# Output rows of the cosine layer in three runs a step instead of seven, and the softmax guard as a sum over column pairs

## Chip, cores and metric

One core of a Trainium2 chip. The metric is the device time of one execution in microseconds (us), the median of three runs. Engines: TensorE (PE, its weight loads are listed as PEld), VectorE (DVE), ScalarE (ACT), GpSimd (POOL), and SyncE (SP), which issues nearly all DMAs.

## The reference, cut to what matters

Windowed attention with 4 batches, 8 heads, 576 tokens and head size 64, then two feed-forward layers over the 2304 tokens of width 512:

```
scores = scale * q @ k.T + slope_h * -|i - j|   (only 0 <= i - j < 128, else -1e9)
e      = exp(scores - max(scores))
x      = (e / (sum(e) + 1e-9)) @ v
g      = x @ w_gate;  x = (g * sigmoid(g) * (x @ w_val)) @ w_out      (d_ff 1536)
h      = x @ w_in;    x = (h * cos(h)) @ w_out2                       (d_ff 2048)
```

All inputs are float32.

## The kernel before

Every float32 operand of the two layers is split in a high and a low part, and each product is three matmuls (high by high, high by low, low by high) that accumulate in PSUM (`mm3`, lines 83 to 86, and `prod`, lines 1009 to 1017). The order in which instructions are issued is written out by hand; each engine then works off its own list in that order and waits for the others by semaphores.

There are three stages.

**Attention** (loop of line 680). Work goes by items (a head and a block of 128 queries), mostly two to a group. For a group the scores are made on PE (`do_s`), bias and row minimum on DVE (`do_bias`, line 514), the exponential with its row sum on ACT (`do_exp`, line 523), then on DVE the guard, which adds 1e-9 to the sum (`do_guard`, line 529), and the reciprocal (`do_recip`, line 534); POOL scales the rows (`do_norm`, lines 546 and 547), PE transposes them (lines 556 and 566) and multiplies by v (line 624). A small tile `st` of 12 columns, one of eight that take turns, holds a group's statistics: columns 0 and 1 the row minima of its one or two items, columns 2 and 4 the sums of exp, column 3 what the tile was filled with at the start (1.0). The guard writes columns 5 to 7 from 2 to 4, the reciprocal columns 8 to 10. Between these steps matmuls of the first layer are issued on PE as filler (lines 84 to 86), and DVE, ACT and POOL split weights for it (line 167 on POOL).

**The rest of the first layer** (loop of line 1062), matmuls of 384 columns without a pause. The last lines of it also set up the third stage.

**The cosine layer** (loop of line 1222), which the change is about. The tokens are in 3 strips of 768 (two halves of `BW` = 384), the 2048 hidden channels in 8 pairs of 128-channel blocks per strip; a step `k` is one pair of one strip, 24 steps (`K2`). h of a step is a 2 by 2 block product, made with seven products (Winograd's form of Strassen's scheme) instead of eight. A slot `m` of the step is one product: six matmuls of 384 columns into a PSUM bank (`prod`). The pool `pm` has two banks; a product takes the one that was let go first. Product 6 accumulates on the bank of product 4 (`p7`), after DVE has read that one once. `take` then reads the product's bank: for m = 0 ACT copies it (line 1166); for all others DVE adds it to an earlier partial sum (line 1156). Products 1, 4, 5 and 6 each give a finished quarter of h, tile `c`, in which a chain begins (`cosine`, lines 1127 to 1147):

- ACT rounds h / 2 pi (two instructions, lines 1130 and 1131)
- DVE subtracts the multiple of 2 pi (two, lines 1134 and 1135)
- ACT takes absolute value and sine (lines 1137 and 1138)
- POOL multiplies by h (line 1140)
- ACT makes the high part `hh` (line 1144), DVE the low part `hl` (line 1146)

Each slot moves every live chain on by one of these parts (`slot_chains`, line 1149; two chains at most while k < 2), then issues what was put off (`flush`), one operation of the next strip's preparation if there is one (`bg`, from `make_xt`, lines 969 to 991: 18 operations, twice in the run, seven of each 18 on DVE, four on POOL), then `take`.

Behind `take` come the output rows. An output row (`out_rows`, line 1191) is g @ w_out2 for 128 tokens and one channel block: three matmuls of 512 columns (lines 84 to 86 again) that accumulate in one of six PSUM banks over all 16 blocks of a strip. A step has 12 rows, 2 blocks by 6 token groups, and those issued in step k belong to step k - 2. `PER` says how many rows stand behind each product:

```
PER = [2, 2, 2, 2, 2, 1, 1]
```

So PE alternates between products and rows seven times a step. There are no rows in steps 0 and 1, and no products in the two steps behind the last (24 and 25), which run rows alone. Behind the last row of a bank's strip, ACT (in the last strip also DVE) copies the bank out, and SP stores it. SP loads a product's weights (`load_ws`) seven products ahead and w_out2's (`load_wo`, in slot 1) about two steps ahead.

Of the kernel before, what the change touches and what calls it, by code (L numbers as in the profile page):

```python
# [13 lines left out]
ALU = mybir.AluOpType  # L14
# [14 lines left out]
def kernel(  # L29
# [12 lines left out]
    nc = tc.nc  # L42
# [165 lines left out]
    def flush():  # L208
        for _ in range(len(post)):
            post.popleft()()  # L210
# [213 lines left out]
        nc.vector.memset(t, 0.0)  # L424
    stats = [const.tile([128, 12], F32, name=f"st{j}") for j in range(8)]
    for t in stats:
        nc.vector.memset(t, 1.0)
    stat_turn = [0]
    pth = {}
    slopes = [2.0 ** (-8.0 * (h + 1) / H) for h in range(H)]  # L430
# [37 lines left out]
    for u in range(U):  # L468
# [4 lines left out]
        for j in range(0, NI, 2):  # L473
            g = list(range(u * NI + j, u * NI + min(j + 2, NI)))
# [4 lines left out]
    def width(i):  # L479
        return 128 if i == 0 else 192 if i == NB else 256  # L480
# [44 lines left out]

    def do_guard(g):
        st = ST[g[0]][0]
        c = 2 * len(g) - 1
        nc.vector.tensor_scalar(st[:, 5:5 + c], st[:, 2:2 + c], 1e-9, None, ALU.add)

    def do_recip(g):
        st = ST[g[0]][0]
        c = 2 * len(g) - 1
        nc.vector.reciprocal(out=st[:, 8:8 + c], in_=st[:, 5:5 + c])  # L534

    def folded(n):

        u, _, i = items[n]
        return u >= NP and i < NB

    def do_norm(n):
        w = width(items[n][2])
        (st, m), e = ST.pop(n), E[n]
        if folded(n) and w == 256:
            w = 128
            nc.gpsimd.tensor_tensor(out=e[:, :w], in0=e[:, :w], in1=e[:, w:2 * w], op=ALU.add)
        nc.gpsimd.tensor_scalar(e[:, :w], e[:, :w], st[:, 8 + 2 * m:9 + 2 * m], 1.0, ALU.mult, ALU.mult)  # L547

    def do_t(g):
        u, h, i = items[g[0]]  # L550
# [129 lines left out]
    for n in range(N + PVS + 2):  # L680
# [19 lines left out]
        if ended(NORM):  # L700
            do_guard(ended(NORM))
        if turned:
            do_t(turned)
        if v1 is not None:
            if idx == TT0:
                g = turned
                prep_tail_t(v1, TT[g[0]] if g else ps_t.tile([128, 512], F32, tag="t", name="t"))
        if ended(NORM):
            do_recip(ended(NORM))
            for m in ended(NORM):  # L710
                do_norm(m)
# [283 lines left out]
    K2 = NS * NPAIR  # L995
# [5 lines left out]
    def load_ws(upto):  # L1001
        while wnext[0] < min(upto, 7 * K2):
            k, m = divmod(wnext[0], 7)
            t = wsp[0].tile([128, 2, 256], F32R, tag="ws", name="ws")
            nc.sync.dma_start(out=f32(t), in_=wid[k % NPAIR][:, m])
            WS[k, m] = t
            wnext[0] += 1

    def prod(k, m, ps, start=True):
        w = WS.pop((k, m))  # L1010
        hi, lo = (x[m] for x in XT[k // NPAIR])
        for kk in range(2):
            c = slice(kk * 128, (kk + 1) * 128)
            o, wh, wl, xh_, xl_ = ps[:, :BW], w[:, 0, c], w[:, 1, c], hi[:, kk], lo[:, kk]
            nc.tensor.matmul(out=o, lhsT=wh, rhs=xh_, start=start and kk == 0, stop=False, skip_group_check=True)  # L1015
            nc.tensor.matmul(out=o, lhsT=wh, rhs=xl_, start=False, stop=False, skip_group_check=True)  # L1016
            nc.tensor.matmul(out=o, lhsT=wl, rhs=xh_, start=False, stop=kk == 1, skip_group_check=True)  # L1017
# [81 lines left out]
    def new_bank(n):  # L1099

        if n < 12 and n % 3:
            return pl2.tile([128, 512], F32, tag="l2", name="l2")
        return pm.tile([128, 512], F32, tag="pm", name="pm")
# [23 lines left out]
    def cosine(k, fi, half, h):  # L1127

        a = ap_.tile([128, BW], F32, tag="a", name="a")
        nc.scalar.activation(out=a, in_=h, func=AF.Copy, scale=INV2PI, bias=MAGIC)  # L1130
        nc.scalar.activation(out=a, in_=a, func=AF.Copy, bias=-MAGIC)
        yield
        r = rp.tile([128, BW], F32, tag="r", name="r")
        nc.vector.scalar_tensor_tensor(out=r, in0=a, scalar=-C1, in1=h, op0=ALU.mult, op1=ALU.add)
        nc.vector.scalar_tensor_tensor(out=r, in0=a, scalar=-C2, in1=r, op0=ALU.mult, op1=ALU.add)  # L1135
        yield
        nc.scalar.activation(out=r, in_=r, func=AF.Abs)  # L1137
        nc.scalar.activation(out=r, in_=r, func=AF.Sin, bias=halfpi, scale=-1.0)  # L1138
        yield
        nc.gpsimd.tensor_tensor(out=r, in0=r, in1=h, op=ALU.mult)  # L1140
        yield
        hi = hp.tile([128, BW], F32R, tag="hh", name="hh")
        lo = hp.tile([128, BW], F32R, tag="hl", name="hl")
        nc.scalar.copy(out=hi, in_=r)
        yield
        nc.vector.tensor_tensor(out=lo, in0=r, in1=f32(hi), op=ALU.subtract)
        HS[k, fi, half] = hi, lo

    def slot_chains(most):

        for c in list(live)[:most]:
            if next(c, "end") == "end":
                live.remove(c)

    def add(out, a, ps):
        nc.vector.tensor_tensor(out=out, in0=ps[:, :BW], in1=a, op=ALU.add)  # L1156
# [3 lines left out]
    def take(k, m, ps):  # L1160

        def new(pool, tag):
            return pool.tile([128, BW], F32, tag=tag, name=tag)
        if m == 0:
            cur["q"] = new(tp, "q")
            nc.scalar.copy(out=cur["q"], in_=ps[:, :BW])  # L1166
        elif m == 1:
            c = new(cp, "c")
            add(c, cur["q"], ps)
            live.append(cosine(k, 0, 0, c))  # L1170
        elif m == 2:
            add(cur["q"], cur["q"], ps)
        elif m == 3:
            cur["r"] = new(tp, "r5")
            add(cur["r"], cur["q"], ps)
        else:
            c = new(cp, "c")
            fi, half, base = {4: (1, 1, "r"), 5: (0, 1, "r"), 6: (1, 0, "q")}[m]
            add(c, cur[base], ps)
            live.append(cosine(k, fi, half, c))  # L1180

    def load_wo(k):
        if k < K2:
            for fi in range(2):
                t = wop.tile([128, 2, 512], F32R, tag="wo", name="wo")
                nc.sync.dma_start(out=f32(t), in_=wod[2 * (k % NPAIR) + fi])
                WO[k, fi] = t
# [3 lines left out]
    def out_rows(k, fi, j):  # L1191

        s, p = divmod(k, NPAIR)
        first, final = p == 0 and fi == 0, p == NPAIR - 1 and fi == 1
        if first:
            sums[j] = (pl2.tile([128, 512], F32, tag="l2", name="l2") if j < 5 else
                       pl1a.tile([128, 512], F32, tag="l1", name="l1"))
        hi, lo = HS[k, fi, j // 3]
        w = WO[k, fi]
        c = slice(j % 3 * 128, (j % 3 + 1) * 128)  # L1200
        mm3(sums[j], hi[:, c], lo[:, c], w[:, 0], w[:, 1], first, final)
        if final:
            def ev(ps=sums[j], row=s * 6 + j):
                o = op_.tile([128, 512], F32, tag="o", name="o")
                if j % 2 and s == NS - 1:
                    nc.vector.tensor_copy(out=o, in_=ps)
                else:
                    nc.scalar.copy(out=o, in_=ps)
                nc.sync.dma_start(out=out[row * 128:(row + 1) * 128, :], in_=o)
            post.append(ev)  # L1210
# [3 lines left out]
    def load_raw(s):  # L1214
        raws[s] = raw_p.tile([128, KD, SB], F32, tag="raw", name="raw")
        nc.sync.dma_start(out=raws[s], in_=y2d[s])

    PER = [2, 2, 2, 2, 2, 1, 1]
    rows = deque()
    bg = deque()  # L1220
    p7 = None
    for k in range(K2 + 2):
        if k >= 2:
            pairs = [(fi, j) for fi in range(2) for j in range(6)]
            rows += [(k - 2, fi, j) for fi, j in (sorted(pairs, key=lambda x: x[1]) if k == K2 + 1 else pairs)]
        for m in range(7):
            if k < K2:
                if k == 0 and m < 2:
                    ps = bank0[m]
                elif m == 6:  # L1230
                    prod(k, m, p7, start=False)
                    ps = p7
                else:
                    ps = new_bank(7 * k + m)
                    prod(k, m, ps)
                if m == 4:
                    p7 = ps
            slot_chains(2 if k < 2 else 99)
            flush()
            if bg:  # L1240
                bg.popleft()()
            if k < K2:
                take(k, m, ps)
            for _ in range(PER[m]):
                if rows:
                    out_rows(*rows.popleft())
            if k < K2:
                load_ws(7 * k + m + 8)
            if m == 1:
                load_wo(k - 1 if k else K2)  # L1250
            s, p = divmod(k, NPAIR)
            if k == 1 and m == 3:
                load_raw(1)
            if m == 3 and s + 1 < NS and p == 3:
                bg += make_xt(s + 1, xta if s % 2 else xtb, raws[s + 1])
            if m == 3 and s + 2 < NS and p == 6:
                load_raw(s + 2)
# [34 lines left out]
```

## Time and profile before

| | |
|---|---|
| median of three runs | 987.6 us (986.79 to 988.35) |
| the profiled execution, time | 984.71 us |
| the profiled execution, span from first to last instruction | 983.0 us |
| mean granted TensorE clock | 0.995 |
| PE busy | 959.1 us, 98% of the span |
| DVE busy | 737.8 us, 75% |
| ACT busy | 593.6 us, 60% |
| POOL busy | 477.9 us, 49% |

Busy time is the time in which an engine has at least one instruction in work. Matmuls overlap (one of 512 columns shows 390 to 397 ns while the next begins after 230), so what a matmul costs in a stream is read from the distance of two starts, not from its duration. In time: attention fills the first 225 us, the first layer runs to about 602 us, the cosine layer from there to the end; its steps with products and rows, k = 2 to 23, lie between 616 and 962 us.

### The profile page before, as it was taken

Reading aid. Unit: us, or ns where it says so; the run is one execution under the profiler, and the core shown is the slowest. Engines: PE = TensorE matmul, PEld = TensorE weight load, DVE = VectorE, ACT = ScalarE, POOL = GpSimd, SP = SyncE. Lnnn points to the kernel's source line nnn. Section 1 sums busy time; section 2 is a strip of 40 time slices with the busy share of each in tenths; the row PEclk is TensorE's granted clock in tenths of the full one; section 3 lists DMA queues with packets and bytes.
Section 4 is the critical chain, followed back from the end, with each engine's and each line's share of the span. In section 5 each row is a group of like instructions: output and inputs, shape, how many; then the busy total and the mean of one; then the engine's idle time right before and its main releaser. Section 6 shows DMA issues by size and latency. Waiting matters only on the chain.

```text
span 983.0 us, 17050 instructions
## 1 busy us (share of the span) xinstructions
PE 959.1 (98%) x5620; PEld 881.3 (90%) x5620; DVE 737.8 (75%) x1553; ACT 593.6 (60%) x1366; POOL 477.9 (49%) x563
## 2 busy tenths in 40 slices
PE   6889999999999999999999999999999999999998
PEld 4568888889999999999999999888989898898886
DVE  6877777766298989989989665799666896666664
ACT  6986566653254545455555334878677776777663
POOL 5766555543155668669578620344232442323221
PEclk8999999999999999999999999999999999999999
DMA  7641433322473547458457625855767656676552
GB/s 182 159 116 42 100 94 87 74 70 68 138 269 111 190 130 258 165 158 250 150 189 240 204 75 174 286 194 190 239 202 231 197 164 201 185 245 200 166 181 86
DMA packets 145159, 163.65 MB, mean 166 GB/s; under 512 B 64688, under 2 KB 105648, under 8 KB 144816
## 3 DMA queue, kind: packets, MB, share of 16 engines
q1 hardware_dynamic: 143872, 162.27, 52.8%
q8 instruction: 45, 0.74, 0.3%
q10 hardware_dynamic: 1200, 0.30, 0.1%
q14 instruction: 42, 0.34, 0.1%
HBM read 126.88 MB, written 35.65 MB: 165 GB/s over the span
## 4 chain that ended last, share of the span: by engine, by line
PE 88%; DVE 5%; ACT 3%; issue 1%; DMA 1%; POOL 1%; SPq 1%; POOLq 0%; DVEq 0%; ACTq 0%
PE l L86 13%; PE l L85 13%; PE l L84 13%; PE pm L84 8%; PE pm L85 8%; PE pm L86 8%; PE pm L1016 5%; PE pm L1017 5%; PE pm L1015 5%; PE s L506 3%; PE pv L624 2%; PE pq L443 1%; PE t L556 1%; PE t L566 1%; DVE e L514 1%
## 5 line engine op out<-in xcount | busy, mean ns | idle before, releaser
L1140 POOL TENSOR_TENSOR r<-r,c 128x384 f32<-128x384 f32 x96 | 104.5, 1090 | 260.5 <-ACT r L1138 168.7
L84 PE MATMUL pm<-xh,wh 128*128 128x384 f32 (+3 forms) x452 | 151.6, 335 | 2.0 <-ACT fu L263 2.0
L85 PE MATMUL pm<-xl,wh 128*128 128x384 f32 (+3 forms) x452 | 144.4, 319 | 0.0
L86 PE MATMUL pm<-xh,wl 128*128 128x384 f32 (+3 forms) x452 | 144.3, 319 | 0.0
L86 PE MATMUL l<-wo,hl 128*128 128x512 f32 x288 | 114.2, 397 | 0.0
L85 PE MATMUL l<-wo,hh 128*128 128x512 f32 x288 | 113.8, 395 | 0.0
L84 PE MATMUL l<-wo,hh 128*128 128x512 f32 x288 | 112.0, 389 | 0.0
L836 POOL TENSOR_TENSOR cs<-cs,st 128x512 uint32<-128x512 uint32 x56 | 79.8, 1425 | 57.3 <-DVE cs L834 47.7
L1016 PE MATMUL pm<-xl,ws 128*128 128x384 f32 x318 | 107.5, 338 | 0.0
L1015 PE MATMUL pm<-xh,ws 128*128 128x384 f32 x318 | 106.5, 335 | 0.6 <-ACT q L1166 0.6
L1017 PE MATMUL pm<-xh,ws 128*128 128x384 f32 x318 | 106.9, 336 | 0.0
L547 POOL TENSOR_SCALAR e<-e,st 128x128 f32<-128x128 f32 (+1 forms) x144 | 60.7, 424 | 62.5 <-DVE st L534 44.7
L84 PEld LDWEIGHTS pm<-xh,wh 128*128 128x128 f32 x452 | 85.1, 188 | 6.4 <-issue 2.7
L85 PEld LDWEIGHTS pm<-xl,wh 128*128 128x128 f32 x452 | 85.2, 188 | 0.0
L86 PEld LDWEIGHTS pm<-xh,wl 128*128 128x128 f32 x452 | 84.9, 188 | 0.0
L1130 ACT ACTIVATE a<-c 128x384 f32<-128x384 f32 x96 | 49.7, 518 | 53.6 <-DVE c L1156 53.6
L523 ACT ACTIVATE e<-e,st 128x256 f32<-128x256 f32 (+1 forms) x144 | 68.0, 474 | 19.0 <-DVE st L514 13.6
L1135 DVE SCALAR_TENSOR_TENSOR r<-a,r 128x384 f32<-128x384 f32 x96 | 76.1, 792 | 3.3
L1137 ACT ACTIVATE r<-r 128x384 f32<-128x384 f32 x96 | 50.4, 525 | 42.3 <-DVE r L1135 42.3
L84 PE MATMUL l<-uh,wh 128*128 128x384 f32 x216 | 72.6, 336 | 0.7 <-DVE acc L961 0.7
L86 PE MATMUL l<-uh,wl 128*128 128x384 f32 x216 | 72.2, 334 | 0.0
L85 PE MATMUL l<-ul,wh 128*128 128x384 f32 x216 | 72.2, 334 | 0.0
(178 smaller groups left out, 2609.5 us busy)
## 6 DMA issues: line engine op xcount, KB each, us to landing
ws<-wid SPq DMA_DIRECT2D x168, 256.0 KB, 2.8
wo<-wod SPq DMA_DIRECT2D x48, 512.0 KB, 5.2
st<-in_moe_w_out_dram SPq DMA_DIRECT2D x28, 512.0 KB, 3.9
st<-in_moe_w_in_dram SPq DMA_DIRECT2D x16, 512.0 KB, 3.7
st<-in_moe_w_gate_dram SPq DMA_DIRECT2D x12, 512.0 KB, 3.9
st<-in_moe_w_val_dram SPq DMA_DIRECT2D x12, 512.0 KB, 3.9
wid<-sh SPq DMA_DIRECT2D x24, 256.0 KB, 4.0
wid<-sl SPq DMA_DIRECT2D x24, 256.0 KB, 3.5
```

The lines of the kernel that those rows point to most:

```text
L84: nc.tensor.matmul(out=ps, lhsT=ah, rhs=bh, start=start, stop=False)
L85: nc.tensor.matmul(out=ps, lhsT=ah, rhs=bl, start=False, stop=False)
L86: nc.tensor.matmul(out=ps, lhsT=al, rhs=bh, start=False, stop=stop)
L523: nc.scalar.activation(out=e[:, :w], in_=e[:, :w], func=AF.Exp, bias=st[:, m:m + 1], scale=-1.0, accum_out=st[:, 2 + 2 * m:3 + 2 * m])
L547: nc.gpsimd.tensor_scalar(e[:, :w], e[:, :w], st[:, 8 + 2 * m:9 + 2 * m], 1.0, ALU.mult, ALU.mult)
L836: nc.gpsimd.tensor_tensor(out=ti, in0=ti, in1=st[:, :, 0], op=ALU.add)
L1015: nc.tensor.matmul(out=o, lhsT=wh, rhs=xh_, start=start and kk == 0, stop=False, skip_group_check=True)
L1016: nc.tensor.matmul(out=o, lhsT=wh, rhs=xl_, start=False, stop=False, skip_group_check=True)
L1017: nc.tensor.matmul(out=o, lhsT=wl, rhs=xh_, start=False, stop=kk == 1, skip_group_check=True)
L1135: nc.vector.scalar_tensor_tensor(out=r, in0=a, scalar=-C2, in1=r, op0=ALU.mult, op1=ALU.add)
L1137: nc.scalar.activation(out=r, in_=r, func=AF.Abs)
L1140: nc.gpsimd.tensor_tensor(out=r, in0=r, in1=h, op=ALU.mult)
```

## The change

The rows stand behind the second, fourth and seventh product (`PER`), four each time. So that product 6 need not wait long for the read of product 4's bank, `take` of product 4 is issued ahead of the slot's chains, from step 2 on; its chain then moves on in the same slot already, one slot earlier than before. In the attention the fill of `st` is 1e-9 in place of 1.0, and the guard adds columns 2 and 3 (and 4 and 5) by one `tensor_reduce`, with the results in columns 6 and 7; the reciprocal takes two columns in place of three.

```diff
     for t in stats:
-        nc.vector.memset(t, 1.0)
+        nc.vector.memset(t, 1e-9)
...
     def do_guard(g):
         st = ST[g[0]][0]
-        c = 2 * len(g) - 1
-        nc.vector.tensor_scalar(st[:, 5:5 + c], st[:, 2:2 + c], 1e-9, None, ALU.add)
+        c = len(g)
+        nc.vector.tensor_reduce(out=st[:, 6:6 + c], in_=st[:, 2:2 + 2 * c].rearrange("p (m t) -> p m t", t=2),
+                                op=ALU.add, axis=mybir.AxisListType.X)

     def do_recip(g):
         st = ST[g[0]][0]
-        c = 2 * len(g) - 1
-        nc.vector.reciprocal(out=st[:, 8:8 + c], in_=st[:, 5:5 + c])
+        c = len(g)
+        nc.vector.reciprocal(out=st[:, 8:8 + c], in_=st[:, 6:6 + c])
...
-        nc.gpsimd.tensor_scalar(e[:, :w], e[:, :w], st[:, 8 + 2 * m:9 + 2 * m], 1.0, ALU.mult, ALU.mult)
+        nc.gpsimd.tensor_scalar(e[:, :w], e[:, :w], st[:, 8 + m:9 + m], 1.0, ALU.mult, ALU.mult)
...
-    PER = [2, 2, 2, 2, 2, 1, 1]
+    PER = [0, 4, 0, 4, 0, 0, 4]
...
                 if m == 4:
                     p7 = ps
+            ahead = 2 <= k < K2 and m == 4
+            if ahead:
+                take(k, m, ps)
             slot_chains(2 if k < 2 else 99)
             flush()
             if bg:
                 bg.popleft()()
-            if k < K2:
+            if k < K2 and not ahead:
                 take(k, m, ps)
             for _ in range(PER[m]):
                 if rows:
```

## Rows read from the trace of the kernel before

**Rows 1.** Page, the chain that ended last: shares of the span by engine

```profile
PE 88%; DVE 5%; ACT 3%; issue 1%; DMA 1%; POOL 1%; SPq 1%; POOLq 0%; DVEq 0%; ACTq 0%
```

**Rows 2.** Windows: length, busy us of PE, PEld, DVE, ACT, POOL; clock, DMA share

```profile
20.00:60.00 40.00, 35.11 (x230) 24.30 (x229) 35.16 (x122) 36.02 (x111) 30.99 (x43) 0.89 0.59 152
...
640.00:960.00 320.00, 320.00 (x1593) 287.72 (x1592) 230.62 (x381) 228.47 (x454) 104.63 (x90) 1.00 0.62 198
```

**Rows 3.** Timeline of PE in one step: first matmul of each run (start, duration)

```profile
693.46 0.39 PE L84 MATMUL l<-wo,hh 128*128 128x512 f32 x1
...
694.16 0.33 PE L1015 MATMUL pm<-xh,ws 128*128 128x384 f32 x1
...
695.22 0.39 PE L84 MATMUL l<-wo,hh 128*128 128x512 f32 x1
...
696.98 0.39 PE L84 MATMUL l<-wo,hh 128*128 128x512 f32 x1
...
698.37 0.33 PE L1015 MATMUL pm<-xh,ws 128*128 128x384 f32 x1
...
699.41 0.39 PE L84 MATMUL l<-wo,hh 128*128 128x512 f32 x1
```

**Rows 4.** Timeline of PE behind the last product: matmuls 1, 13 and 25 of rows

```profile
961.90 0.39 PE L84 MATMUL l<-wo,hh 128*128 128x512 f32 x1
...
964.66 0.39 PE L84 MATMUL l<-wo,hh 128*128 128x512 f32 x1
...
967.38 0.39 PE L84 MATMUL l<-wo,hh 128*128 128x512 f32 x1
```

**Rows 5.** Timeline of DVE: the read of the product whose rows begin at 693.46

```profile
693.66 0.56 DVE L1156 TENSOR_TENSOR c<-pm,r 128x384 f32<-128x384 f32 x1 [1.30 <-PE pm L1017]
```

**Rows 6.** Lines, 640 to 960 us: busy us, mean ns | idle before; DVE, then ACT

```profile
L1135 DVE SCALAR_TENSOR_TENSOR r<-a,r 128x384 f32<-128x384 f32 x81 | 66.2, 817 | 2.8
L1146 DVE TENSOR_TENSOR hl<-r,hh 128x384 fp32r<-128x384 f32 x83 | 52.0, 627 | 0.0
L1134 DVE SCALAR_TENSOR_TENSOR r<-a,c 128x384 f32<-128x384 f32 x81 | 46.9, 579 | 4.4 <-ACT a L1131 4.4
L1156 DVE TENSOR_TENSOR c<-pm,r 128x384 f32<-128x384 f32 x41 | 22.8, 556 | 42.6 <-PE pm L1017 42.6
...
L981 DVE TENSOR_TENSOR xl<-raw,xh 128x768 fp32r<-128x768 f32 x10 | 10.2, 1020 | 0.0
...
L1131 ACT ACTIVATE a<-a 128x384 f32<-128x384 f32 x82 | 43.1, 526 | 2.6
...
L1130 ACT ACTIVATE a<-c 128x384 f32<-128x384 f32 x81 | 42.0, 518 | 48.1 <-DVE c L1156 48.1
```

**Rows 7.** Timelines of PE, ACT and DVE in step 2

```profile
617.35 0.39 PE L84 MATMUL l<-wo,hh 128*128 128x512 f32 x1
...
621.38 0.46 ACT L1166 COPY q<-pm 128x384 f32<-128x384 f32 x1
...
622.86 0.55 DVE L1156 TENSOR_TENSOR c<-pm,q 128x384 f32<-128x384 f32 x1
...
628.60 0.55 DVE L1156 TENSOR_TENSOR r<-pm,q 128x384 f32<-128x384 f32 x1
...
632.44 0.55 DVE L1156 TENSOR_TENSOR c<-pm,r 128x384 f32<-128x384 f32 x1
...
633.04 0.45 PE L1015 MATMUL pm<-xh,ws 128*128 128x384 f32 x1
```

**Rows 8.** Lines 529 (guard) and 534 (reciprocal): duration ns least/median/most

```profile
L529 DVE TENSOR_SCALAR st<-st x80: 143/166/1112, 11.8 to 211.8; 128x3 f32<-128x3 f32 x64, 128x1 f32<-128x1 f32 x16
...
L534 DVE RECIPROCAL st<-st x80: 162/176/178, 12.1 to 212.0; 128x3 f32<-128x3 f32 x64, 128x1 f32<-128x1 f32 x16
```

**Rows 9.** The chain that ended last near 28 us; POOL's timeline there

```profile
27.54 0.56 DVE st L529
...
28.48 1.10 POOL L547 TENSOR_SCALAR e<-e,st 128x128 f32<-128x128 f32 x2 [0.41 <-DVE st L534]
```

## The prediction

> **What bounds the kernel now.** First the chain of waits: 88% of it is PE [rows 1]. Then the windows: in the cosine layer PE is busy for all of 320 us, with DVE and ACT at 231 and 228 [rows 2]. So there a change counts only if PE's stream gets shorter or gets a hole. In the early attention PE has 35.1 busy of 40 us, DVE 35.2 and ACT 36.0 [rows 2]: there a chain over several engines sets the pace, and a shorter DVE instruction can count.
>
> Next, PE's timeline, for what a switch between products and rows costs. I read distances between starts. A single row takes 0.70 (693.46 to 694.16), the product behind it 1.06; a pair of rows 1.39, the product behind it 1.04 [rows 3]. Behind the last product rows run without a switch: the first 12 matmuls take 2.76, the next 12 take 2.72 [rows 4]. A settled row is therefore 2.72 / 4 = 0.68, and every switch adds a few hundredths, which long runs pay less often.
>
> **The change, part by part.** Durations are those of the profiled execution, 984.71 us with a span of 983.0; the median of the runs is 2.9 higher, and I put the difference on the median.
>
> *Switches.* A step before: five pairs and two singles, 5 x 1.39 + 2 x 0.70, with five products of 1.04 and two of 1.06: 15.67 us. After: three runs like the first of [rows 4] and seven products of 1.04: 3 x 2.76 + 7 x 1.04 = 15.56. That is 0.11 a step, and 2.3 over the 21 steps from 3 to 23 (step 2 comes below). No row shows a product behind a run of twelve matmuls. If it were 1.06, as behind a single, the step would gain 0.05, and all of them 1.1; if the switch into it were free, 0.13 and 2.7. I take 1.04, from the pair, the nearest run in length.
>
> *The waits that products have on reads.* Count from the start of a step's product 0. Product 4 ends at 4 x 1.04 + 2 x 2.76 + 1.04 = 10.72, product 5 at 11.76, product 6 at 12.80, the rows at 15.56. Product 6 overwrites the bank of product 4, so it must wait for its read. DVE begins such a read 0.20 behind the end of the product (693.46 to 693.66) and needs 0.56 [rows 3, 5]; PE started 0.05 behind the end of a read on which it waited (632.99 to 633.04) [rows 7]. So product 6 may start at 10.92 + 0.56 + 0.05 = 11.53, and PE comes to it at 11.76: 0.23 to spare, if DVE is free at 10.92. Ahead of that read stand product 3's read (0.56), chain 0's pair (0.58 + 0.82) and in some steps one operation of the preparation (1.02), 2.98 in all [rows 6]; product 3 is seen at 7.12, so there are 3.8 us for them. That is why I cost this wait at nothing; if the cover is gone, it is the slow rival below.
>
> Behind the read DVE has two `hl` (2 x 0.63), then the pair of chain 1 (1.40), which also waits for ACT's two (0.52 + 0.53, done at about 12.5), then the reads of products 5 and 6 [rows 6]: 11.48 + 1.26 + 1.40 + 0.56 = 14.70 and 15.26. The next step's product 0 takes the bank of product 5, at 15.56, 0.8 to spare; product 1 takes that of 6 at 16.60, 1.3 to spare. So an ordinary step has no wait. Twice in the run the preparation of a strip adds a DVE operation of 1.02 [rows 6] to slot 4 and another to slot 6 of one step, and one to slot 5 of the step before it. Then the reads end at 15.72 and 17.30: product 0 is 0.2 late, product 1 (due at 16.8) 0.55, the step before it 0.1, and each hole costs 0.1 more, since the matmul behind one shows 0.45 against 0.33 [rows 3, 7]. That is 1.1 a strip. L1135's mean of 0.82, beside 0.58 for L1134, holds some long ones; with 0.56 in its place 0.5 is left. I take 0.6, nearer to the low end, as no large POOL operation falls in those slots: +1.2 for two strips, between 0 and 2.2.
>
> *Step 2* starts with ACT behind: it works off the chains of steps 0 and 1 without a pause, so the reads stay where they are. Product 0 ends at 617.35, product 1 then at 618.39, four rows at 621.15. Product 2 waits for ACT's copy until 621.84 (as before), and ends at 623.04 with its slow start. Product 3 needs the bank that DVE reads until 623.41: 0.43 late, end 624.6. Rows to 627.4, product 4 to 628.4. Product 5 needs product 3's bank, read until 629.15: 0.8 late, end 630.35. Product 6 and four rows end at 634.15, where the next step began at 633.04 before [rows 7]. So +1.2, between 0 (ACT's backlog gets shorter) and 1.5. The two rows behind each product covered these waits before.
>
> *The guard.* Undisturbed it takes 166 ns, but up to 1112; the reciprocal, next to it on the same tile, never over 178 [rows 8]. On the chain near 28 us the guard stands with 0.56, and POOL, done with its own work, then idles 0.41 until the reciprocal lets it go on [rows 9]: the guard ended only when POOL's instruction did. If the new reduction takes about 0.17 at any time, like the reciprocal, guard and reciprocal are over while POOL still works, and the idle time falls to some 0.03. I find three such places on the chain before 64 us (near 28, 40 and 58): 3 x 0.38 = -1.1. Later PE is the bound and the rest is hidden. The bounds: no gain, and 0.17 lost at each place if the reduction costs double (+0.5); two more held guards in that stretch just beside the chain (-2.0). I take the reciprocal as the nearest row. The Trainium skill says why (SBUF — State Buffer, Who interferes with whom): VectorE and GpSimd share a port pair under an exclusive lock, `tensor_scalar` can enter a mode that needs it, and `tensor_reduce` on trn2 never contends. By that rule the -1.1 stands; the two ranges of duration agree with it for the guard, and no row here has a reduction.
>
> *At nothing:* the fill's value, two columns in place of three in the reciprocal, POOL's scalar column (same instructions as before). SP issues the same loads in the same order; a product's weights are still asked for seven products ahead, and w_out2's behind the rows of slot 1 for the step after. At a strip's end four of the six copies out come together in slot 0 on ACT, ahead of the copy that frees product 0's bank; product 2 needs that bank at 4.84 only, and the cover would cost twice some tenths. Chain 1 moves one slot earlier, which its own work in [rows 6] has room for. Behind the last product 28 rows stand instead of 25, with 16 ahead of the last step's in place of 13: the last chains have more cover.
>
> **The sum:** -2.3 + 1.2 + 1.2 - 1.1 = -1.0. Against the profiled execution 983.7, on the median 986.6.
>
> **The rivals.**
> - *Faster, 0.27.* The waits of step 2 and of the preparations don't come, since DVE and ACT run ahead: -2.3 - 1.1 = -3.4, 984.2. For it: DVE has 90 us idle in 320 [rows 2]. Against it: its work is in order, and in step 2 the reads hang on ACT.
> - *Slower, 0.13.* Product 6 waits in every step. Its place is the read of product 4, its point 0.23 us of lateness. If one `hl` (0.63) is still ahead of it, the hole is 0.63 - 0.23 + 0.1 = 0.5, over 21 steps 10.5, and the time 997. For it: DVE's long L1135; against it: 3.8 us for 3.0 of work.
> - *The change doesn't do what it says, 0.10.* The excess of 0.02 to 0.03 belongs to what other engines do in the middle steps, not to the switch, and long runs keep it. Then the switches give 0, and the sum is +1.3: 988.9. For it: the only settled rows are from a stretch without products. Against: they begin with the same three or so slow matmuls.
> - *The reduction is dear, 0.05.* It takes twice the guard's 0.17: +0.5 instead of -1.1, 988.2. The Trainium skill has a rule that way (VectorE: DVE Perf Modes, Rules for kernel authors): `tensor_reduce` on the hot path is the slowest VectorE operation, better restructured. Nothing here shows one; for four columns I expect the fixed cost, which [rows 8] give.
>
> **How the numbers follow.** The forecast itself has 0.45. What can be told from no change is about 0.2%, 2 us: below 985.6 is faster, above 989.6 slower. Of the forecast's 0.45, 0.09 fall below 985.6 by its bounds and 0.02 above 989.6; of the third rival 0.03 lie above. Faster 0.27 + 0.09 = 0.36; slower 0.13 + 0.02 + 0.03 = 0.18; same 0.46. The terms' best ends give -2.7 - 2.0 and some wait, near -4.2: 983.4. The worst give -1.1 + 2.2 + 1.5 + 0.5 = +3.1, 990.7; I put the upper end at 990.5, and leave out the slow rival.
>
> **What would show it.** Switches: twelve row matmuls in 2.76 and a step of 15.56 from product 0 to product 0. Product 6: its first matmul starts 1.04 behind product 5's, not later, in all steps. Preparations: holes before products 0 and 1 in one step of each of the first two strips, and nowhere else past step 2. Step 2: product 3 at 623.5 and product 5 at 629.2 (less what the attention gained). Guard: a longest duration near 0.2 and no idle time of 0.4 on POOL behind the reciprocal. The prediction is wrong if holes recur in every step, or if the row runs keep 0.695 a row.

## The result, and the profile after

The kernel became slower: 992.63 us (median of 8 runs, 990.05 to 995.41) beside 987.91 (8 runs, 986.74 to 988.89) for the kernel before on the same chip. The ratio is 1.0052, with a 95% interval from 1.0038 to 1.0066, so 4.7 us more (3.8 to 6.5). The forecast was 986.6, and its range ended at 990.5.

| | before | after |
|---|---|---|
| the profiled execution, time / span | 984.71 / 983.0 us | 993.04 / 991.3 us |
| mean granted TensorE clock | 0.995 | 0.994 |
| PE's share of the chain that ended last | 88% [rows 1] | 83% |
| third stage, first product's start to last matmul's start | 598.16 to 978.72 = 380.56 us | 600.46 to 987.04 = 386.59 us |
| behind the last matmul's start | 4.3 us | 4.3 us |

The row of the third stage is the one to read first: it splits the difference of the two spans (8.3 us) into the third stage (+6.0) and all that precedes it (+2.3). The start of the third stage cannot be put down to the change: over the eleven kernels profiled here it lies between 598.1 and 603.1, among those with the old guard (598.2, 598.1, 601.1) as among those with the new one (598.3 to 603.1). So below I compare stage lengths, which repeat far better, and take whole times from the medians only.

Line numbers behind the guard (line 529) are one higher in the kernel after. Page of the kernel after, the chain that ended last (answers to [rows 1]):

```profile
PE 83%; DVE 7%; ACT 5%; DMA 2%; issue 2%; POOL 1%; SPq 0%; DVEq 0%; POOLq 0%; ACTq 0%
```

DMA's share rose from 1% to 2%: some transfer is now waited for. The windows of the kernel after, as in [rows 2]:

```profile
20.00:60.00 40.00, 35.03 (x223) 24.03 (x219) 33.33 (x120) 35.68 (x109) 30.27 (x43) 0.91 0.54 147
...
640.00:960.00 320.00, 315.76 (x1567) 282.66 (x1566) 215.64 (x377) 223.69 (x451) 102.08 (x90) 1.00 0.61 198
```

PE was busy for all of these 320 us before and now lacks 4.2. The waits in the same stretch name what it lacked them for (columns: us in total, times, longest):

```profile
ACT o L1209 <- DMA out_dram<-o: 5.8, 2, 3.0
...
PE pm L1016 <- ACT q L1167: 3.5, 2, 1.9
...
PE pm L1016 <- DVE c L1157: 0.4, 2, 0.2
PE pm L1016 <- DVE r L1157: 0.4, 2, 0.2
```

Two large holes lie behind ACT's copy of product 0, four small ones behind reads of DVE. There was no such PE wait in this stretch before. Now the places. PE at the first of the large ones, with an ordinary step ahead of it:

```profile
712.94 0.39 PE L84 MATMUL l<-wo,hh 128*128 128x512 f32 x1
...
715.70 0.33 PE L1016 MATMUL pm<-xh,ws 128*128 128x384 f32 x1
...
717.80 0.39 PE L84 MATMUL l<-wo,hh 128*128 128x512 f32 x1
...
751.62 0.39 PE L86 MATMUL l<-wo,hl 128*128 128x512 f32 x1
753.59 0.44 PE L1016 MATMUL pm<-xh,ws 128*128 128x384 f32 x1 [1.58 <-ACT q L1167]
```

The first three lines are an ordinary step: twelve row matmuls in 2.76 (712.94 to 715.70) and the two products behind them in 2.10. The last two are a strip's end: from the last row matmul to product 2 it takes 1.97, where 0.23 is normal. The other strip end has 2.28 (product 2 at 881.89). ACT at the first of them:

```profile
743.91 1.06 ACT L1209 COPY o<-l 128x512 f32<-128x512 f32 x2
...
748.30 1.54 ACT L1209 COPY o<-l 128x512 f32<-128x512 f32 x3
752.57 0.58 ACT L1209 COPY o<-l 128x512 f32<-128x512 f32 x1 [2.73 <-DMA out_dram<-o]
753.05 0.48 ACT L1167 COPY q<-pm 128x384 f32<-128x384 f32 x1
```

Two of the strip's six output rows are copied out together, 4.4 us later the other four. Three of these copies go through; the fourth stands 2.73 us, because the pool `op` has three output tiles and the fourth copy needs that of the first of the four, whose store has not landed. Behind it in ACT's list is the copy that frees product 0's bank, and product 2 needs that bank. (Stores land 2.0 us after their issue at the least and 4.2 at the most; before, 2.0 and 3.6.)

The small holes: PE, DVE and POOL in step 4, where the next strip is prepared.

```profile
657.86 0.34 PE L1018 MATMUL pm<-xh,ws 128*128 128x384 f32 x1
658.39 0.45 PE L1016 MATMUL pm<-xh,ws 128*128 128x384 f32 x1 [0.19 <-DVE c L1157]
```

```profile
654.16 0.95 DVE L982 TENSOR_TENSOR xl<-raw,xh 128x768 fp32r<-128x768 f32 x1
...
656.09 1.77 DVE L982 TENSOR_TENSOR xl<-raw,xh 128x768 fp32r<-128x768 f32 x1
657.79 0.55 DVE L1157 TENSOR_TENSOR c<-pm,q 128x384 f32<-128x384 f32 x1
...
660.59 2.61 DVE L982 TENSOR_TENSOR raw<-raw 128x768 f32<-128x768 f32 x1
663.12 0.54 DVE L1157 TENSOR_TENSOR r<-pm,q 128x384 f32<-128x384 f32 x1
```

```profile
656.02 1.03 POOL L1141 TENSOR_TENSOR r<-r,c 128x384 f32<-128x384 f32 x1 [2.78 <-ACT r L1139]
...
660.25 2.13 POOL L982 TENSOR_TENSOR xl<-raw,xh 128x768 fp32r<-128x768 f32 x1 [1.52 <-ACT xh L985]
```

The start of product 3 comes 0.53 behind the matmul ahead of it instead of 0.17, since the read of product 1 stands behind a DVE operation of the preparation that took 1.77, not 1.02 [rows 6]. The second, before product 5, is behind one of 2.61. Both times the DVE operation began while POOL worked on SBUF operands, and ended 0.8 behind POOL's end (657.05 and 662.38). From 640 us on DVE has 14 operations of the preparation: the six that began so took 1.77 (four) or 2.61 (two) and ended 0.8 behind POOL, the eight others took 0.95, as the one at 654.16. Step 12 repeats the pair. In step 2 two more holes came, before products 3 and 5, as forecast:

```profile
625.73 0.44 PE L1016 MATMUL pm<-xh,ws 128*128 128x384 f32 x1 [0.24 <-DVE c L1157]
...
631.49 0.44 PE L1016 MATMUL pm<-xh,ws 128*128 128x384 f32 x1 [0.60 <-DVE r L1157]
```

The account of the third stage, from distances of starts (a matmul behind a hole is followed after 0.28 instead of 0.17, so each hole costs 0.1 more than its length):

| | worked out | us |
|---|---|---|
| two strip ends | 1.97 + 2.28 - 2 x 0.23 + 2 x 0.1 | +4.0 |
| steps 4 and 12 | 4 x (0.53 - 0.17 + 0.1) | +1.8 |
| step 2 | 0.40 + 0.77 + 0.2, less some 0.3 for a hole that only the kernel before had | +1.05 |
| switches in 21 steps | 21 x (15.64 - 15.69) | -1.05 |
| sum | beside +6.0 measured | +5.8 |

The 0.2 that are left lie in steps 6 and 14, which took 15.75 each and not 15.64.

The guard and the reciprocal after (answers to [rows 8]; duration ns least/median/most), and POOL near 28 and 36 us (answers to [rows 9]):

```profile
L529 DVE TENSOR_REDUCE st<-st x80: 140/151/159, 12.2 to 214.5; 128x2 f32<-128x4 f32 x64, 128x1 f32<-128x2 f32 x16
```

```profile
27.86 1.26 POOL L548 TENSOR_SCALAR e<-e,st 128x128 f32<-128x128 f32 x2
...
35.59 0.42 POOL L548 TENSOR_SCALAR e<-e,st 128x192 f32<-128x192 f32 x1 [2.18 <-DVE st L535]
```

The long guards (up to 1112 ns) are gone, and so is POOL's idle time of 0.41 near 28 us. At 35.6 POOL waits 2.18 for the reciprocal; in the kernel before the same instruction waited 1.67:

```profile
35.94 0.43 POOL L547 TENSOR_SCALAR e<-e,st 128x192 f32<-128x192 f32 x1 [1.67 <-DVE st L534]
```

So a part of what was won at one place seems to be waited for at the next.

### The profile page after: what moved, and what is told of

The parts are those of the page before. It is cut to its first block, busy times and chain, and to the rows that moved or that the text cites. A ratio compares the mean times of both kernels' runs of the same rounds, so it can differ in the third digit from the quotient of the medians.

```text
span 991.3 us, 17071 instructions
## 1 busy us (share of the span) xinstructions
PE 963.3 (97%) x5620; PEld 883.0 (89%) x5620; DVE 718.1 (72%) x1553; ACT 590.9 (60%) x1366; POOL 475.6 (48%) x563
## 4 chain that ended last, share of the span: by engine, by line
PE 83%; DVE 7%; ACT 5%; DMA 2%; issue 2%; POOL 1%; SPq 0%; DVEq 0%; POOLq 0%; ACTq 0%
PE l L84 12%; PE l L85 12%; PE l L86 12%; PE pm L84 8%; PE pm L85 8%; PE pm L86 8%; PE pm L1016 5%; PE pm L1018 5%; PE pm L1017 5%; PE s L506 4%; PE pv L625 3%; PE pq L443 1%; PE t L557 1%; DVE cs L834 1%; DMA out_dram<-o 1%
## 5 line engine op out<-in xcount | busy, mean ns | idle before, releaser
L1141 POOL TENSOR_TENSOR r<-r,c 128x384 f32<-128x384 f32 x96 | 101.2, 1059 | 269.7 <-ACT r L1139 192.0
L1135 DVE SCALAR_TENSOR_TENSOR r<-a,c 128x384 f32<-128x384 f32 x96 | 60.1, 626 | 28.4 <-ACT a L1132 27.9
```

## Experiments

Each kernel ran beside the kernel before on the same chip. "Stage" is the length of the third stage, first product to last matmul: 380.56 before, 386.59 after.

**1. The guard alone** (the kernel before with the fill of 1e-9, the `tensor_reduce`, the two-column reciprocal and POOL's scalar column; the rows as before):

```diff
-        nc.vector.tensor_scalar(st[:, 5:5 + c], st[:, 2:2 + c], 1e-9, None, ALU.add)
+        nc.vector.tensor_reduce(out=st[:, 6:6 + c], in_=st[:, 2:2 + 2 * c].rearrange("p (m t) -> p m t", t=2),
+                                op=ALU.add, axis=mybir.AxisListType.X)
```

> The guard's half of the change alone, rows as before. Theory: the reduction takes 0.15 us always (no instance over 0.2), and frees POOL 0.3 to 0.4 us sooner at three places before 64 us, so the time is 0.3 to 1.5 us below the kernel before (ratio 0.9985 to 1.000), the third stage's length unchanged at 380.6 us from its first product to the last matmul. Rival: the 2.3 us by which the third stage began later in the profiled run of the changed kernel come from the guard, by stretches at the half clock that its new timing brings; then this kernel is about 2.3 us slower than before (ratio 1.002 to 1.003).

Measured: 986.75 (12 runs) beside 987.17 (29 runs), ratio 0.9994 [0.9983, 1.0006]; stage 380.50. The guard took 142 to 157 ns. So the guard costs 0.6 us at the most, and its gain cannot be told from no change: -0.6 us, between -1.7 and +0.6. The 4.7 us are not its.

**2. The rows alone** (the kernel before with the new `PER` and the early read; old guard):

```diff
-    PER = [2, 2, 2, 2, 2, 1, 1]
+    PER = [0, 4, 0, 4, 0, 0, 4]
...
+            ahead = 2 <= k < K2 and m == 4
...
```

> The order of rows and products alone, guard as before. Theory: all of the loss is here: third stage 386.6 us from first product to last matmul (6.0 longer than before), time 5 to 6.5 us above before (ratio 1.005 to 1.0065). Rival (the guard costs 2.3): the stage is longer by 6.0 all the same, but then guard and rows together would have to give 8 us, and the whole change's 4.7 us contradicts it; under it this kernel is only 2 to 3 us slower than before (ratio 1.002 to 1.003).

Measured: 993.08 (6 runs), ratio 1.0055 [1.0035, 1.0076]. The whole loss is here. The stage was 384.99, with the six small holes in their places at 0.52 to 0.95. That is 1.6 less than expected, since the strip ends differed from each other and cost 2.3 in all, where the profiled execution after has 4.0. ACT there:

```profile
750.37 0.58 ACT L1208 COPY o<-l 128x512 f32<-128x512 f32 x1 [2.82 <-DMA out_dram<-o]
...
876.93 0.59 ACT L1208 COPY o<-l 128x512 f32<-128x512 f32 x1 [1.24 <-DMA out_dram<-o]
```

Where the store was waited for 2.82, PE had a hole of 2.07; where it was waited for 1.24, one of 0.49. The hole follows the store's landing one to one (1.58 and 1.58), which speaks for the output tile and against ACT's load as its cause.

**3. A fourth output tile** (the kernel after with one more tile in `op`):

```diff
-    op_ = sc.enter_context(tc.tile_pool(name="op", bufs=3, reuse_waits="tile"))
+    op_ = sc.enter_context(tc.tile_pool(name="op", bufs=4, reuse_waits="tile"))
```

> The changed kernel with a fourth buffer for the output tiles that ACT copies out at a strip's end. Theory: the sixth copy no longer waits for the store of the third, so ACT's copy that frees product 0's bank comes in time, the holes of 1.97 and 2.28 us before product 2 at the two strip ends are gone, and the third stage is 3.8 us shorter than the changed kernel's, 382.8 us; time 3.5 to 4.2 us below it, within 1.2 us of before. Rival: ACT's four copies in a bunch (2.3 us) are enough by themselves to make the copy late; then holes of 0.5 to 1 us stay at these places and the gain is 2 to 3 us.

Measured: 988.49 (12 runs), ratio 1.0014 [1.0004, 1.0025]; stage 382.64, so 3.95 shorter than after. ACT and PE at the strip's end:

```profile
747.73 2.03 ACT L1209 COPY o<-l 128x512 f32<-128x512 f32 x4
...
749.62 0.51 ACT L1167 COPY q<-pm 128x384 f32<-128x384 f32 x1
```

```profile
751.26 0.33 PE L1016 MATMUL pm<-xh,ws 128*128 128x384 f32 x1
```

The four copies run through, and product 2 comes without idle time. This one number accounts for 4.0 of the 6.0 us in the stage. The medians say nearly the same: ratios of 1.0052 and 1.0014 to the kernel before are 3.8 us apart. The six small holes stayed, 0.52 to 0.95 between starts. Experiments 4, 5, 6 and 8 build on this kernel.

**4. Short runs in the steps with holes** (experiment 3, with the old `PER` and no early read in steps 2, 4 and 12):

```diff
+    LONG, SHORT = [0, 4, 0, 4, 0, 0, 4], [2, 2, 2, 2, 2, 1, 1]
+    short = {2, 4, NPAIR + 4}
...
-            for _ in range(PER[m]):
+            for _ in range((SHORT if k in short else LONG)[m]):
```

> As the one with four buffers, and in steps 2, 4 and 12 the old order (rows behind every product). Theory: the holes of step 2 (0.57 and 0.94 us gaps) and of steps 4 and 12 (two gaps of 0.53 us each) come from reads that the two rows behind each product covered, and go with them; the rest gains 0.05 us a step over 19 steps: third stage 379.7 us, about 0.9 below the kernel before, time with the guard 0.5 to 2 us below before (ratio 0.998 to 0.9995). Rival: DVE and ACT are behind in those steps by their own amount of work, so the hole moves to the next long step (5 or 13, or 3); then the stage stays at 381.5 us or more.

Measured: 987.13 (12 runs), ratio 1.0003 [0.9992, 1.0014]; stage 380.96, between the 379.7 expected and the rival's 381.5. The holes moved to the long steps behind the short ones (PE):

```profile
636.54 0.44 PE L1016 MATMUL pm<-xh,ws 128*128 128x384 f32 x1 [0.21 <-DVE c L1157]
...
673.25 0.44 PE L1016 MATMUL pm<-xh,ws 128*128 128x384 f32 x1 [0.25 <-DVE c L1157]
```

One in step 3, one in step 5, one in step 13 (0.54, 0.59 and 0.37 between starts). This fits a lateness of DVE that is carried into the next step and shows where rows no longer stand behind each product.

**5. Without the early read** (experiment 3 with the read of product 4 back behind the chains):

```diff
-            ahead = 2 <= k < K2 and m == 4
+            ahead = False
```

> Four buffers, and the read of product 4 issued behind the slot's chains again. Theory (DVE has time to spare ahead of that read): the chain operation that then stands ahead of it is done before product 4 ends, so ordinary steps stay at 15.64 us without a hole before product 6; chain 1 starts one slot later, and the stage grows by at most 1 us from 382.6. Rival: the read comes 0.6 us late and product 6 waits 0.4 us in each of 21 steps, 16.1 us a step and a stage of 391 us.

Measured in one execution: 987.56, stage 382.41. PE, and the read of product 4:

```profile
723.88 0.33 PE L1016 MATMUL pm<-xh,ws 128*128 128x384 f32 x1
...
727.03 0.39 PE L84 MATMUL l<-wo,hh 128*128 128x512 f32 x1
```

```profile
725.14 0.56 DVE L1157 TENSOR_TENSOR c<-pm,r 128x384 f32<-128x384 f32 x1 [1.85 <-PE pm L1018]
```

Products 4 to 6 pass in 3.15 without a hole: DVE waits for the product here, not the product for DVE. In an ordinary step the early read isn't needed, and the rival of product 6 waiting in every step has no ground.

**6. Two runs a step** (experiment 3 with six rows each behind products 3 and 6):

```diff
-    PER = [0, 4, 0, 4, 0, 0, 4]
+    PER = [0, 0, 0, 6, 0, 0, 6]
```

> Four buffers, and the rows in two runs of six a step, behind products 3 and 6. Theory: a run of rows has 0.04 us over its settled time whatever its length, and the first product behind a long run 0.026, so a run fewer gives 0.067: 15.57 us a step where nothing waits (against 15.64 with three runs, 15.69 with seven). What it loses by products 2 and 3 waiting for the reads of 0 and 1 shows as holes there, 0.1 to 1 us in each step. Rival: the excess grows with the run's length, then a step without holes is 15.63 us or more.

Measured in one execution: 1004.55, stage 395.46. An undisturbed step takes 15.58 (4.12 twice for the rows, 3.15 and 4.19 for the products), 0.06 less than with three runs. The holes expected in every step did not come. Larger ones did: of 3.69 us in step 2, of 2.43 and 2.44 at the strip ends, and of 0.80 to 1.47 in steps 4 to 6 and 12 to 14, at the preparations. Two stretches show a lower granted clock, one without holes does not (windows; last columns clock, DMA share, GB/s):

```profile
620.00:640.00 20.00, 16.55 (x75) 14.61 (x76) 13.55 (x28) 15.88 (x34) 6.54 (x7) 0.91 0.82 306
700.00:740.00 40.00, 40.00 (x202) 36.16 (x201) 24.36 (x48) 25.17 (x51) 9.77 (x10) 1.00 0.61 203
885.00:905.00 20.00, 17.90 (x82) 15.90 (x81) 9.80 (x20) 13.38 (x28) 4.03 (x4) 0.91 0.66 223
```

**7. Six pairs** (the kernel before with its two singles made a pair, so that only one run falls away):

```diff
-    PER = [2, 2, 2, 2, 2, 1, 1]
+    PER = [2, 2, 2, 2, 2, 2, 0]
```

> The kernel before with the last row of the step moved from behind product 6 to behind product 5 (2, 2, 2, 2, 2, 2, 0): six pairs of rows instead of five pairs and two singles. Theory: by the prices read from the trace (a single 0.040 us over settled time with the product behind it, a pair 0.034) a step falls from 15.69 to 15.64, without taking cover from any read, so the stage falls by 1.0 us from 380.6 to 379.6, and the time by about 1 us (ratio 0.998 to 0.9995). Rival: product 0 stands right behind product 6 and meets a read that comes late; then a hole of 0.2 us or more recurs there and the stage is 381 us or more.

Measured: 988.2 (12 runs) beside 987.13 (17 runs), ratio 1.0011 [1.0001, 1.0021]; stage 381.20. A step takes 15.64, as priced, yet new holes of 0.77 and 0.78 in steps 4 and 12 ate the gain (one of 0.42 in step 3 has its like, 0.46, in the kernel before). The first of them, PE and DVE:

```profile
664.48 0.44 PE L1015 MATMUL pm<-xh,ws 128*128 128x384 f32 x1 [0.37 <-DVE r L1156]
```

```profile
660.84 2.24 DVE L1135 SCALAR_TENSOR_TENSOR r<-a,r 128x384 f32<-128x384 f32 x1
663.01 0.95 DVE L981 TENSOR_TENSOR raw<-raw 128x768 f32<-128x768 f32 x1
663.88 0.54 DVE L1156 TENSOR_TENSOR r<-pm,q 128x384 f32<-128x384 f32 x1
```

The kernel before holds the same instruction as long, in the same step:

```profile
657.17 2.24 DVE L1135 SCALAR_TENSOR_TENSOR r<-a,r 128x384 f32<-128x384 f32 x1
...
660.20 0.55 DVE L1156 TENSOR_TENSOR r<-pm,q 128x384 f32<-128x384 f32 x1
```

There it began 8.34 behind the start of the step's product 0 (648.83), and the read ended 0.26 ahead of product 5; in this run it began 9.16 behind (651.68), and the read came too late. So the cover of the kernel before was just enough, and moving one row lost it in the preparation's steps; why DVE came to the instruction later is open.

**8. The preparation behind the read** (experiment 3 with the `bg` operation moved behind `take`):

```diff
-            if bg:
-                bg.popleft()()
             if k < K2 and not ahead:
                 take(k, m, ps)
+            if bg:
+                bg.popleft()()
```

> Four buffers, and in each slot the preparation's operation issued behind the read of the product instead of ahead of it. Theory: the gaps of 0.53 us before products 3 and 5 of steps 4 and 12 come from a preparation operation that DVE has ahead of the reads of products 1 and 3 (1.8 and 2.6 us long there, held up by POOL); with the order turned, the four gaps go and the stage is 382.6 - 4 x 0.46 = 380.8 us. Rival: DVE is behind by its sum of work in these steps; then the gaps come up at other products and the stage stays above 382 us.

Measured in one execution: 989.2, stage 381.75. The four holes of 0.53 are gone, and two of 0.62 came in steps 6 and 14. PE and DVE at the first:

```profile
690.81 0.45 PE L1016 MATMUL pm<-xh,ws 128*128 128x384 f32 x1 [0.28 <-DVE c L1157]
```

```profile
686.43 2.21 DVE L1135 SCALAR_TENSOR_TENSOR r<-a,c 128x384 f32<-128x384 f32 x1
```

So the preparation's operation ahead of the read did make those four holes; what is left again has an instruction of a chain that took 2.21 in place of 0.58 in front of it.

**9. The best of the parts on the kernel before** (new guard, six pairs, preparation behind the read):

```diff
-    PER = [2, 2, 2, 2, 2, 1, 1]
+    PER = [2, 2, 2, 2, 2, 2, 0]
...
-            if bg:
-                bg.popleft()()
             if k < K2:
                 take(k, m, ps)
+            if bg:
+                bg.popleft()()
```

> What the runs so far point to: six pairs of rows (2, 2, 2, 2, 2, 2, 0), the preparation's operation issued behind the read of the product, and the new guard. Theory: a step without a hole is 15.64 us; the two gaps of 0.77 us that six pairs alone had before product 5 of steps 4 and 12 come from the preparation's operation ahead of the read of product 3 and go; only the two gaps of step 2 and 3 that the kernel before also has are left. Stage 379.6 us, 1.0 below the kernel before, and 0.3 to 0.8 from the guard: ratio 0.998 to 0.999. Rival: DVE, held up 2.2 us by POOL in those steps, is late whatever the order; then gaps of 0.5 us or more stay in steps 4 to 6 and 12 to 14 and the stage is 380.5 us or more, the time the same as before.

Measured: 986.55 (11 runs) beside 987.53 (15 runs), ratio 0.9994 [0.9984, 1.0004]; stage 380.83. The holes moved one step on (0.77 and 0.76, in steps 5 and 13). No version here can be told to be faster than the kernel before.

## Why the prediction was wrong, point by point

**Strip-end copies: the step that failed.** They were costed "at nothing", with the sentence that "the cover would cost twice some tenths". They cost 4.0 (3.95 taken back by one more tile), more than all other terms together. The four copies were seen to come together on ACT, ahead of the copy that frees product 0's bank, and product 2's need of it at 4.84 was right too. What was not counted was what the copies themselves need: a free output tile. With six copies in two groups of two and four, three tiles, and a store that lands 2.0 to 4.2 us after its issue, the fourth copy waits for DMA. Before, the six copies came in four slots (two, two, one, one), and at these two strip ends none waited for a store.

**Switches: the direction right, the size half.** Twelve row matmuls take 2.76 as forecast. But the two products behind them take 2.106, not 2.08: the first one needs 1.066. That was named as a bound ("if it were 1.06 ... all of them 1.1"), and the pair was chosen as the nearest run in length, which was the wrong neighbour. Its 1.04 is also no more than six settled product matmuls take (6 x 0.1733), so the way into a product was priced at nothing. A step went from 15.69 to 15.64, so -1.05 in all, not -2.3. The third rival falls (the excess belonging to other engines and not to the switch): the step shortens each time that a run falls away, 15.69, 15.64, 15.58 for seven, three and two runs.

**Preparations: holes foreseen, at the wrong place and too small.** They came, in one step of each strip, but before products 3 and 5 and not before products 0 and 1, with 1.84 instead of 1.2 (and inside the bound of 2.2). The forecast followed the preparation's operations in slots 4 to 6 only, at 1.02 each and with 0.56 for a chain's, "as no large POOL operation falls in those slots". Those that did the harm stand in slots 1 and 3 of step 4, ahead of the reads of products 1 and 3, and took 1.77 and 2.61 beside POOL's 1.03 and 2.13. The Trainium skill has the rule (SBUF — State Buffer, Who interferes with whom): a DVE instruction with two SBUF inputs contends with a GpSimd instruction that reads SBUF, through the shared read port. The trace agrees: the six that began beside such a POOL instruction ended 0.8 us behind it, and the eight others took 0.95. No run here took POOL's work away, so the cause of the length is read from this, not tested.

**Step 2: right.** Waits before products 3 and 5 of 0.40 and 0.77 beside 0.43 and 0.8 forecast; +1.05 in all beside +1.2.

**Product 6: right.** It waited in no ordinary step, not even without the early read (experiment 5), so the slow rival didn't happen; the kernel is slower for another reason than the one that was priced for that side.

**Guard: the mechanism right, its worth not settled.** The longest guard fell from 1112 to 159 ns and POOL's 0.41 near 28 us went, as forecast. Whether the -1.1 came cannot be told: experiment 1 gives -0.6, and its interval (-1.7 to +0.6) holds -1.1 as well as nothing; the two kernels with the rows changed (after and experiment 2) differ by 0.45, far less than either spreads. The sum took three places as independent; the trace shows POOL's wait for the reciprocal at 36 us longer by 0.51 than before. That the time is given back along that chain is argued from this one place, not shown. The dear reduction falls: 151 ns in the median beside the guard's 166.

With what was measured in the profiled executions, the forecast's own sum would have been -1.05 + 1.05 + 1.84 + 4.0 for the stage, +5.8, and about -0.5 for the guard: +5.3, inside the measured 3.8 to 6.5.

## What to carry to other kernels

When short pieces of work are bunched into longer ones, list what else was spread out with them: here the copies of finished rows, each of which needs an output tile until its store has landed, so a bunch of four with three tiles put 2 us of DMA onto the critical path twice. The short runs of rows were also cover: the two rows behind a product gave its read time, also when DVE was held (1.8 to 2.6 us in one instruction). Without them such reads came late in three steps, and these holes (1.05 + 1.8) cost more than the fewer switches gave (1.05). Price a switch from runs of the length that is planned, or take the bound on the unfavourable side as the forecast.

## What the runs showed of the hardware that was not expected

**A switch does not cost the same for every run.** From a settled matmul (0.2267 us for rows, 0.1733 for products) a step of 36 row and 42 product matmuls would take 15.44. Measured are 15.69 with seven short runs, 15.64 with three of twelve matmuls and 15.58 with two of eighteen: an excess of 0.036, 0.067 and 0.07 us for each run and the products behind it. A run of three or six matmuls is thus half as dear as a longer one, and from twelve to eighteen the length made no difference. Why is open.

**A small reduction is the safe form of a guard.** In 80 instructions `tensor_reduce` took 140 to 159 ns, also beside a working POOL (the first of 24 to 40 us starts at 27.28, in POOL's subtraction of 26.60 to 27.87), where `tensor_scalar` took up to 1112 [rows 8].

```profile
27.28 0.14 DVE L529 TENSOR_REDUCE st<-st 128x2 f32<-128x4 f32 x1
```

```profile
26.60 1.27 POOL L167 TENSOR_TENSOR wl<-ct,wh 128x512 fp32r<-128x512 f32 x1 [0.47 <-ACT wh L174]
```

The Trainium skill's rule that `tensor_reduce` on a hot path is the slowest VectorE operation (VectorE: DVE Perf Modes, Rules for kernel authors) does not hold for four columns by these numbers; that it never contends on trn2 (SBUF — State Buffer, Who interferes with whom) they agree with.

**The clock fell behind some holes, and differs by execution.** The eight executions of the kernel after lie between 990.05 and 995.41, with mean granted clocks of 0.989 to 0.997: 0.989 for the two slowest (995.41 and 995.39), 0.997 for the second fastest (990.61), but 0.991 for the fastest, so the clock can be a part of the spread and not all. The landing of the stores may be another part: the strip ends cost 4.0 in one execution (after) and 2.3 in another (experiment 2). The profiled executions show where: of 48 to 70 us the kernel before has 0.92 granted and the kernel after 0.77, while from 12 to 48 it is 0.91 and 1.00 (windows, PE alone, of the kernel after):

```profile
12.00:48.00 36.00, 30.34 (x180) 1.00 0.64 171
48.00:70.00 22.00, 19.55 (x116) 0.77 0.38 92
```

In this early attention, stretches of a few us run at the lower of the two levels (1.2 GHz; granted 0.50 from 48.4 to 55.2 in the kernel after), and they fall at other times in other executions: with the old guard as with the new. What sets their place was not tried. In experiment 6 such stretches came in the third stage as well: behind the hole of 3.69 in step 2 (granted 0.50 from 627.7 to 631.1) and behind the hole of 2.44 at a strip end (0.51 from 890.6 to 894.0). Behind the one of 2.43 at the other strip end the clock stayed at 1.00, and so it did behind all holes of the kernel after in this stage. This is why stage lengths were compared here, and why 0.5 us of the guard could not be told from no change.
